# Attention scores as three float32r products, with TensorE in a written order

## The chip, the cores and the metric

The kernel runs on one core of a Trainium2 chip. That core has five engines with their own instruction queues: TensorE (PE; its weight loads are shown apart as PEld), VectorE (DVE), ScalarE (ACT), GpSimd (POOL) and SyncE (SP), which issues the transfers. [...] The metric is the device time of one execution, in microseconds (us).

## The reference, cut to what matters

```python
# q, k, v: (8 batches, 8 heads, 576, 64)
scores = scale * np.matmul(q, k.transpose(0, 1, 3, 2))
mask = block_i >= block_j                       # blocks of 64
scores = np.where(mask, scores, -1000000000.0)
attn = np.exp(scores - max); attn = attn / (sum + 1e-09)
x = np.matmul(attn, v)                          # heads side by side: (8, 576, 512)

h = gelu(x @ w_in); u, v = halves of h          # 512 columns each
v_n = (v - mu) / np.sqrt(var + 1e-06) * g_ln
v_s = np.einsum('ts,bsd->btd', w_sg, v_n) + b_sg[None, :, None]
out = x + (u * v_s) @ w_out
```

All of it is float32.

## The kernel before, in words

Attention is done for a pair of heads at a time: 32 pairs, four to a batch. `load_qk` brings q and k of a pair with the head's 64 values on the rows, head 0 in rows 0 to 63, head 1 in rows 64 to 127, so that the scores of the two heads are products in the two halves of TensorE's rows. A query tile i (five of them) needs the keys up to its own block only. `Scores` makes the scores in four steps (step1: tile 4's first 288 keys and tile 1's 192; step2: tile 4's other 288; step3: tile 3's 448 and tile 0's 64; step4: tile 2's 320). In each, TensorE writes two PSUM banks, one for each head (tile `s`), VectorE takes mask and row maximum (`maximum`, L297), and ScalarE makes the exponentials (`exponent`, L310) into `prob`. `Values` turns the probabilities (`pa`, `pb`, `pc`, `pd`: transposes through PSUM, copied out to `pt`), multiplies them with v (`ob`), turns the reciprocal sums (`pe`), and `normalise` multiplies. The result x is written to DRAM (`spill`) and split in two float32r parts (`split`: xh, xl).

A batch's four pairs done, the feed-forward part runs in pieces: five value strips (`accv`), eight pieces of u (`accu`), eight spatial (`accs`), eight of the output (`acco`). These products are float32r already: each factor is split in a high and a low part, and three products stand for one. Between the value strips and the spatial pieces lies the normalisation (`moments`, `inverse_std`, `centre`, `scale`) on VectorE and GpSimd.

A slot handles pair n's values, pair n + 1's scores, and some pieces of feed-forward work of the batch before (`hole`). The order in which each engine gets its instructions comes from a scheduler that works from the program order and its own estimate of times; `keep_in_program_order` pins single instructions. [...] The output pieces of a batch stand behind the value and u pieces of the next one (`last_o`). In the order printed by the program below, line 85 is every product and line 88 every transpose. Weights come as 64-bit numbers and are turned to float32 by ScalarE and VectorE (`from_f64`), then split.

Of the kernel before, what the change touches and what calls it, by code (L numbers as in the profile page):

```python
# [16 lines left out]
DRAM = bass.MemoryType.DRAM  # L17

# [9 lines left out]
def kernel(  # L28
# [12 lines left out]
    nc = tc.nc  # L41
# [15 lines left out]
    PIN = ""  # L57
# [6 lines left out]
    KINDS = {"x": ("x", 3), "xr": ("r", 2), "xh": ("y", 4), "xl": ("z", 4)}  # L64
# [24 lines left out]

    def copy(e, dst, src):  # L90
        f = {"v": nc.vector.tensor_copy, "a": nc.scalar.copy, "g": nc.gpsimd.tensor_copy}[e]
        return f(dst, src)  # L92
# [8 lines left out]
    def load_qk(n):  # L101
        b, h = PAIRS[n]
        q_f = sp.tile([P, S], F32, tag="q_f", name="q_f", bufs=2)
        k_f = sp.tile([P, S], F32, tag="k_f", name="k_f", bufs=2)
        nc.sync.dma_start(q_f, qT[b, h : h + 2].rearrange("a d s -> (a d) s"))
        nc.sync.dma_start(k_f, kT[b, h : h + 2].rearrange("a d s -> (a d) s"))
        qk[n] = (q_f, k_f)

    def load_v(n):
        b, h = PAIRS[n]  # L110
        v_f = v_bufs[n % 2]
        cols = slice(h * D, (h + 2) * D)
        nc.sync.dma_start(
            v_f[:, : NT - 1, :],
            v[b, : (NT - 1) * P, cols].rearrange("(j p) d -> p j d", p=P),
        )
        nc.sync.dma_start(v_f[:TAIL, NT - 1, :], v[b, S - TAIL :, cols])
        vals[n] = v_f
# [12 lines left out]
    nc.gpsimd.memset(mask, 0.0)  # L131
    nc.gpsimd.memset(mask[:BLK, MW - BLK :], -8.0e9)
    half = cp.tile([P, NT], F32, name="half")
    nc.gpsimd.memset(half, -0.5)
    stats = cp.tile([P, NT, 2], F32, name="stats")
    nc.gpsimd.memset(stats, 1.0)


    for s in (0, 1):
        t = cp.tile([P, NT, 2 * D], F32, name=f"v_f{s}")  # L140
        nc.gpsimd.memset(t[TAIL:, NT - 1, :], 0.0)
        v_bufs.append(t)
    pt0 = []
    for s in (0, 1):
        t = cp.tile([P, 2 * BLK], F32, name=f"pt0_{s}")
        nc.gpsimd.memset(t[BLK:, :], 0.0)
        pt0.append(t)
    prob = []
    for s in range(4):
        row = []  # L150
        for i in range(NT):
            t = cp.tile([P, P * (i + 1) if i else BLK], F32, name=f"prob{s}_{i}")
            if i:
                nc.gpsimd.memset(t[:, EXT[i] :], 0.0)
# [13 lines left out]
    def split_weight(x, dh, dl):  # L168
        nc.scalar.copy(dh, x)
        nc.gpsimd.tensor_tensor(dl, x, dh.bitcast(F32), op=ALU.subtract)  # L170

    def from_f64(raw, dh, dl):
# [8 lines left out]
        nc.scalar.activation(m.bitcast(F32), hi.bitcast(F32), AF.Abs, scale=2.0**-112)  # L181

        nc.vector.tensor_scalar(t, lo, 29, None, op0=ALU.logical_shift_right)
        nc.vector.scalar_tensor_tensor(
            t, hi, 0x80000000, t, op0=ALU.bitwise_and, op1=ALU.bitwise_or
        )
        nc.vector.scalar_tensor_tensor(
# [4 lines left out]
    def load_weight(src, cols, dh, dl):  # L192
# [5 lines left out]
        def fetch(k):  # L198
            if k < len(parts):
                c, fs = parts[k]  # L200
                raws[k] = page(src.dtype, W, "w")
                nc.sync.dma_start(raws[k], src[c * P : (c + 1) * P, fs])
# [3 lines left out]
        for k, (c, fs) in enumerate(parts):  # L206
            fetch(k + 2)
# [3 lines left out]
            else:  # L211
                from_f64(*args)
            yield True

    def load_spatial():
        nc.sync.dma_start(g_bc, g_ln.unsqueeze(0).broadcast_to([P, DH]))
        t = page(F32, S, "w")
        nc.gpsimd.memset(t[BLK:, :DH], 1.0)
        nc.vector.tensor_copy(vone[BLK:, :], t[BLK:, :DH])
        for j in range(NT - 1):  # L220
            t = page(F32, S, "w")
            nc.sync.dma_start(t, w_sgT[j * P : (j + 1) * P, :])
# [5 lines left out]
        for hf in (0, 1):  # L228
            nc.sync.dma_start(t[hf * BLK : (hf + 1) * BLK, :], w_sgT[j * P : S, :])
        t2 = page(F32, S, "w")  # L230
        nc.gpsimd.memset(t2[BLK:, :], 0.0)
        nc.sync.dma_start(t2[BLK : BLK + 1, :], b_sg.unsqueeze(0))
        nc.sync.dma_start(t2[96:97, :], b_sg.unsqueeze(0))
        nc.scalar.copy(ws_h[:, j, :], t)
        nc.gpsimd.tensor_tensor(
            ws_l[:BLK, j, :], t[:BLK, :], ws_h[:BLK, j, :].bitcast(F32), op=ALU.subtract
        )
        nc.scalar.copy(ws_l[BLK:, j, :], t2[BLK:, :])
        nc.vector.tensor_tensor(
# [27 lines left out]
    class Scores:  # L267


        def __init__(self, n):  # L270
            self.q, self.k = qk.pop(n)
            self.sm = sp.tile([P, NT, 2], F32, tag="sums", name="sums", bufs=3)
            nc.gpsimd.memset(self.sm[:, 0, :], 1.0)  # L273
# [6 lines left out]
        def products(self, *parts):  # L280
# [3 lines left out]
            for i, lo, hi in parts:  # L284
                n, rows = QN[i], slice(0, QN[i])
                for a in (0, 1):
                    r = slice(a * D, (a + 1) * D)
                    dst = t[a][rows, off : off + hi - lo]
                    self.where[a, i, lo] = dst
                    mm(dst, self.q[r, QS[i] : QS[i] + n], self.k[r, lo:hi], start=True, stop=True)  # L290
                off += hi - lo

        def maximum(self, a, i, lo, hi):
# [3 lines left out]
            nc.vector.tensor_tensor_reduce(  # L297
# [10 lines left out]
        def exponent(self, a, i):  # L308
            r, e = slice(0, QN[i]), EXT[i]
            nc.scalar.activation(  # L310
# [8 lines left out]
        def step(self, *parts):  # L319
# [4 lines left out]
            for a in (0, 1):  # L324
                for i, lo, hi in parts:
                    if hi == EXT[i]:
                        self.exponent(a, i)
# [10 lines left out]
        def step4(self):  # L338
            self.step((2, 0, EXT[2]))

    TE = {(0, 0): "a", (1, 0): "v", (0, 2): "a", (1, 2): "v", (0, 1): "a", (1, 1): "a"}

    class Values:
# [45 lines left out]
        def inverse(self):  # L389

            r = sp.tile([P, NT * 2], F32, tag="r", name="r", bufs=2)
            nc.vector.tensor_scalar_add(r, self.sm.rearrange("p i a -> p (i a)"), 1e-9)  # L392
            nc.vector.reciprocal(r, r)
            self.rx = sp.tile([P, NT, 2 * D], F32, tag="rx", name="rx", bufs=1)
            nc.gpsimd.tensor_copy(
# [4 lines left out]
        def turn_sums(self):  # L400
# [4 lines left out]
            turn(t[:, 128:256], self.rx[:, 0, :], ident)  # L405
            pt = self.pt0 = pt0[self.n % 2]
            copy("a", pt[:BLK, :], t[:BLK, : 2 * BLK])
            self.rb = sp.tile([P, S], F32, tag="rb", name="rb")
            copy("a", self.rb[:, :BLK], t[:, 128:192])
            t = pbank("pe")  # L410
            for i in range(1, NT):
                turn(t[:, (i - 1) * P : i * P], self.rx[:, i, :], ident)
            copy("a", self.rb[:, BLK:], t)
# [16 lines left out]
        def av1(self):  # L430
            pt = [self.pt.pop((a, 1)) for a in (0, 1)]
            self.av(self.ob[:, 64:512], 1, pt, 0, 448, False, False)
            self.av(self.ob[:, 448:512], 4, pt, 448, 64, False, True)
            self.o0 = self.t4[:, 256 : 256 + BLK]
# [342 lines left out]
```

## Time and profile before

| | us |
|---|---|
| median of the two runs | 1058.67 |
| the two runs | 1051.1, 1066.24 |
| the profiled execution | 1052.77 |
| its span (first to last instruction) | 1050.8 |
| TensorE busy | 964.7 |
| VectorE busy | 465.9 |
| ScalarE busy | 427.0 |
| GpSimd busy | 267.4 |

Busy times are those of the profiled execution. Matmuls are pipelined, so a busy TensorE is not one at its best rate, and how long one product takes in a row of them is read from start to start. The granted clock is the share of its full speed that TensorE's clock had. "Idle before" and a releaser name whose work ended a wait.

### The profile page before, as it was taken

How to read it: one execution, taken by the hardware profiler on the slowest of the kernel's cores; microseconds unless marked ns; L12 is line 12 of the kernel's file. 1: busy time of each engine (PE TensorE's matmuls, PEld its weight loads, DVE VectorE, ACT ScalarE, POOL GpSimd, SP SyncE). 2: the span in 40 equal slices, each digit the busy share in tenths (PEclk: the TensorE clock that was granted, in tenths of full speed). 3: DMA queues.
4: the chain of work that ended last, by engine and by line, in shares of the span. 5: the costliest groups of instructions: out<-in, count | busy, mean ns of one | idle time of the engine just before them, and what ended most of it. 6: DMA issues, size and time to landing. Idle time of an engine off the chain costs nothing.

```text
span 1050.8 us, 15018 instructions
## 1 busy us (share of the span) xinstructions
PE 964.7 (92%) x5554; PEld 690.3 (66%) x5554; DVE 465.9 (44%) x1442; ACT 427.0 (41%) x1122; POOL 267.4 (25%) x341
## 2 busy tenths in 40 slices
PE   8699999998889988999889998899988999889988
PEld 4245767576657765677666776567765577658978
DVE  6855285427334273342722526434263342723333
ACT  5765662562253622536224263243632536322210
POOL 3621064104212042120420303302042020422232
PEclk7799999998989989899878999889989899869999
DMA  7522111112210122101220112211122011112022
GB/s 233 167 91 68 56 56 46 46 46 68 95 34 31 46 68 90 46 22 46 68 80 34 46 47 68 79 35 46 46 68 88 27 44 58 34 39 75 1 90 68
DMA packets 46908, 65.61 MB, mean 62 GB/s; under 512 B 4082, under 2 KB 22514, under 8 KB 46836
## 3 DMA queue, kind: packets, MB, share of 16 engines
q1 hardware_dynamic: 46836, 64.67, 18.8%
q8 instruction: 43, 0.70, 0.3%
q14 instruction: 29, 0.24, 0.1%
HBM read 45.78 MB, written 18.87 MB: 62 GB/s over the span
## 4 chain that ended last, share of the span: by engine, by line
PE 76%; DVE 13%; ACT 3%; DMA 2%; POOL 2%; issue 2%; SPq 1%; DVEq 0%; POOLq 0%; ACTq 0%
PE s L85 12%; PE accs L85 12%; PE acco L85 11%; PE ob L85 11%; PE accv L85 10%; PE accu L85 9%; PE pc L88 3%; PE pb L88 3%; DVE prob L297 3%; PE pa L88 2%; DVE bs L518 2%; DVE xr L635 2%; ACT prob L310 1%; PE pe L88 1%; DMA w<-in_w_in 1%
## 5 line engine op out<-in xcount | busy, mean ns | idle before, releaser
L310 ACT ACTIVATE prob<-prob,negm 128x448 f32<-128x448 f32 (+3 forms) x320 | 177.8, 556 | 235.5 <-DVE negm L297 234.1
L85 PE MATMUL s<-k_f,q_f 64*128 64x288 f32 (+4 forms) x768 | 193.9, 447 | 34.2 <-DVE negm L297 23.7
L297 DVE CUSTOM_DVE_ANT_0 prob<-s,mask 128x288 f32<-128x288 f32 (+2 forms) x320 | 122.2, 424 | 168.9 <-PE s L85 168.8
L85 PEld LDWEIGHTS s<-k_f,q_f 64*128 64x128 f32 (+1 forms) x768 | 88.9, 188 | 102.1 <-issue 40.3
L85 PE MATMUL ob<-pt,v_f 128*64 128x448 f32 (+4 forms) x640 | 129.5, 454 | 11.0 <-ACT pt L92 6.6
L85 PE MATMUL acco<-gh,wo_h 128*128 128x288 f32 x256 | 94.2, 369 | 19.5 <-DVE xr L635 10.9
L273 POOL MEMSET sums<- 128x2 f32 x32 | 4.3, 137 | 353.1 <-DVE r L392 353.1
L611 POOL TENSOR_TENSOR gl<-u,gh 128x288 fp32r<-128x288 f32 x64 | 51.6, 807 | 154.6 <-DVE gh L610 151.9
L85 PEld LDWEIGHTS ob<-pt,v_f 128*64 128x64 f32 x640 | 44.1, 141 | 69.2 <-issue 39.7
L85 PE MATMUL acco<-gl,wo_h 128*128 128x288 f32 x256 | 87.1, 340 | 0.0
L85 PE MATMUL acco<-gh,wo_l 128*128 128x288 f32 x256 | 86.6, 338 | 0.0
L635 DVE TENSOR_TENSOR xr<-acco,xr 128x288 f32<-128x288 f32 x64 | 29.0, 456 | 121.1 <-PE acco L85 113.5
L85 PEld LDWEIGHTS acco<-gh,wo_h 128*128 128x128 f32 x256 | 58.9, 230 | 31.8 <-DVE xr L635 16.6
L85 PE MATMUL accu<-xh,wi_h 128*128 128x288 f32 x256 | 79.1, 309 | 0.0
L85 PE MATMUL accs<-ws_h,vh 128*128 128x288 f32 x256 | 76.8, 303 | 1.5 <-ACT pt L92 1.5
L85 PE MATMUL accs<-ws_h,vl 128*128 128x288 f32 x256 | 75.9, 297 | 0.0
L85 PE MATMUL accu<-xh,wi_l 128*128 128x288 f32 x256 | 75.5, 295 | 0.0
L85 PE MATMUL accu<-xl,wi_h 128*128 128x288 f32 x256 | 75.4, 295 | 0.0
L85 PE MATMUL accs<-ws_l,vh 128*128 128x288 f32 x256 | 75.1, 294 | 0.0
L85 PE MATMUL accv<-wi_h,xh 128*128 128x512 f32 x160 | 66.0, 413 | 0.0
L92 ACT COPY pt<-pa 128x512 f32<-128x512 f32 x32 | 18.6, 581 | 110.8 <-PE pa L88 110.8
L85 PE MATMUL accv<-wi_l,xh 128*128 128x512 f32 x160 | 63.4, 396 | 0.0
(102 smaller groups left out, 1839.8 us busy)
## 6 DMA issues: line engine op xcount, KB each, us to landing
q_f<-in_qT SPq DMA_DIRECT2D x32, 288.0 KB, 2.9
k_f<-in_kT SPq DMA_DIRECT2D x32, 288.0 KB, 3.2
spill<-x SPq DMA_DIRECT2D x32, 288.0 KB, 3.2
xr<-spill SPq DMA_DIRECT2D x32, 288.0 KB, 2.8
out_T<-xr SPq DMA_DIRECT2D x32, 288.0 KB, 2.1
v_f<-in_v SPq DMA_DIRECT2D x32, 256.0 KB, 3.1
w<-in_w_in SPq DMA_DIRECT2D x16, 256.0 KB, 4.7
w<-in_w_out SPq DMA_DIRECT2D x8, 256.0 KB, 3.9
```

What stands on the lines that cost most here:

```text
L85: return pin(nc.tensor.matmul(*a, **k), "P")
L88: return pin(nc.tensor.transpose(out, in_, identity), "P")
L92: return f(dst, src)
L273: nc.gpsimd.memset(self.sm[:, 0, :], 1.0)
L297: nc.vector.tensor_tensor_reduce(self.prob[a][i][r, lo:hi], self.where[a, i, lo], mask[r, MW - (hi - lo) :] if 0 < i and hi == e else mask ...
L310: nc.scalar.activation(self.prob[a][i][r, :e], self.prob[a][i][r, :e], AF.Exp, bias=self.negm[a][r, i : i + 1], scale=-1.0, accum_out=self ...
L518: tc.keep_in_program_order(nc.vector.bn_stats(bs[:rows, :], x))
L611: nc.gpsimd.tensor_tensor(glo[:, ts], x, ghi[:, ts].bitcast(F32), op=ALU.subtract)
L635: nc.vector.tensor_tensor(x[:, ts], acc[:, :SH], x[:, ts], op=ALU.add)
```

## The change

Scores: q and k of a pair are split on the chip, into a float32r high part (VectorE) and the rest (GpSimd), and the score is three products, high by high, high by low, low by high, in one accumulation. For each product the two heads follow one another. The first pair keeps its one fp32 product. q_f and k_f have one buffer each in place of two, and the split of the pair after next stands at the slot's end, so its transfers and the single q_h, k_h, q_l, k_l follow on the step 4 that read the last ones.

Order: `PIN = "P"` pins every TensorE instruction to program order; the other engines are still scheduled. The slot is written anew: one piece of feed-forward work at seven places (PLAN), each score step between a piece and a product with v, the exponentials after the piece behind their step, the side work (`run_side`) in shares of two and three. A batch's output pieces follow its own spatial pieces in the same four slots; those of the last batch but one stay for the end. ScalarE copies `ob` out of PSUM, and VectorE multiplies it with the turned sums where they lie in PSUM; before, ScalarE copied the sums and VectorE read ob. Weight pieces get a tag of their own with two buffers, shared with xr, and are fetched after the piece before is used; x has two buffers in place of three.

```diff
-    PIN = ""
+    PIN = "P"
...
-    KINDS = {"x": ("x", 3), "xr": ("r", 2), "xh": ("y", 4), "xl": ("z", 4)}
+    KINDS = {"x": ("x", 2), "xr": ("r", 2), "raw": ("r", 2), "xh": ("y", 4), "xl": ("z", 4)}
...
+    def split_qk(n):
+        q_f, k_f = qk[n]
+        parts = []
+        for x, name in ((q_f, "q"), (k_f, "k")):
+            hi = sp.tile([P, S], F32R, tag=name + "_h", name=name + "_h")
+            V.tensor_copy(hi, x)
+            parts.append(hi)
+        for x, name, hi in ((k_f, "k", parts[1]), (q_f, "q", parts[0])):
+            lo = sp.tile([P, S], F32R, tag=name + "_l", name=name + "_l")
+            G.tensor_tensor(lo, x, hi.bitcast(F32), op=ALU.subtract)
+            parts.append(lo)
+        q_h, k_h, k_l, q_l = parts
+        qk[n] = [(q_h, k_h), (q_h, k_l), (q_l, k_h)]
...
         for i, lo, hi in parts:
...
-                    mm(dst, self.q[r, QS[i] : QS[i] + n], self.k[r, lo:hi], start=True, stop=True)
+                for y, (q, k) in enumerate(self.terms):
+                    for a in (0, 1):
+                        r = slice(a * D, (a + 1) * D)
+                        mm(
+                            self.where[a, i, lo],
+                            q[r, cols],
+                            k[r, lo:hi],
+                            start=(y == 0),
+                            stop=(y == len(self.terms) - 1),
+                        )
...
         def normalise(self):
...
-            nc.vector.tensor_tensor(x[:, :BLK], self.o0, self.rb[:, :BLK], op=ALU.mult)
-            nc.vector.tensor_tensor(x[:, BLK:], self.ob, self.rb[:, BLK:], op=ALU.mult)
+            copy("a", x[:, BLK:], self.ob)
+            copy("a", x[:, :BLK], self.o0)
+            V.tensor_tensor(x[:, BLK:], self.rp, x[:, BLK:], op=ALU.mult)
+            V.tensor_tensor(x[:, :BLK], self.t4[:, 128:192], x[:, :BLK], op=ALU.mult)
...
-    WS = [2, 5, 7, 8, 3, 2, 1, 1]
+    WS = [6, 7, 7, 4, 3, 2]
...
-    PLAN = ["12211", "12211", "12211", "12222"]
+    PLAN = ["1111111", "1111111", "1111111", "1111112"]
...
+        va.turn0(0)
+        va.turn0(1)
+        hole(g[0])
+        load_share(n, 0)
+        run_side(2)
         if nx:
             nx.step1()
+        va.av0()
+        if nx:
+            nx.exponents(1)
+        va.turn2(0)
+        va.turn2(1)
+        hole(g[1])
+        run_side(2)
         if nx:
             nx.step2()
+        va.av2()
...
-                work.extend([v_, u_, *last_o, s_])
-                last_o[:] = [o_]
+                if b < B - 2:
+                    work.extend([v_, u_, s_, o_])
+                elif b == B - 2:
+                    work.extend([v_, u_, s_])
+                    last_o.append(o_)
+                else:
+                    work.extend([v_, *last_o, u_, s_, o_])
```

How this moves instructions shows at three places. The first is TensorE at step 3 of a slot in the steady part, before (tile `s` is the scores, one number for each head; `ob` the product with v, `pc` transposes; columns are line, operation, out<-in, shape):

```order
L85 MATMUL s_5259<-k_f_4890,q_f_4889 128x448
L85 MATMUL s_5259<-k_f_4890,q_f_4889 64x64
L85 MATMUL s_5260<-k_f_4890,q_f_4889 128x448
L85 MATMUL s_5260<-k_f_4890,q_f_4889 64x64
L85 MATMUL ob_5240<-pt_5230,v_f0_101 64x512
L88 MATMUL pc_5311<-ident_70,prob0_4_116 128x128
```

The same step in the changed program, on TensorE:

```order
L86 MATMUL s_2790<-k_h_2575,q_h_2573 128x448
L86 MATMUL s_2791<-k_h_2575,q_h_2573 128x448
L86 MATMUL s_2790<-k_l_2577,q_h_2573 128x448
L86 MATMUL s_2791<-k_l_2577,q_h_2573 128x448
L86 MATMUL s_2790<-k_h_2575,q_l_2579 128x448
L86 MATMUL s_2791<-k_h_2575,q_l_2579 128x448
L86 MATMUL s_2790<-k_h_2575,q_h_2573 64x64
L86 MATMUL s_2791<-k_h_2575,q_h_2573 64x64
L86 MATMUL s_2790<-k_l_2577,q_h_2573 64x64
L86 MATMUL s_2791<-k_l_2577,q_h_2573 64x64
```

One head's products stood before the other's; now the heads take turns, product by product, and there are three where there was one.

The second place is GpSimd in the normalisation of a batch's value half, from the power (`rs`) to the last low part (`vl`), before:

```order
L537 TENSOR_TENSOR vv_1041<-vv_1041,rs_1184 64x512
L542 TENSOR_TENSOR vl_1545<-vv_1123,vh_1544 128x512
L537 TENSOR_TENSOR vv_1138<-vv_1138,rs_1184 128x512
L542 TENSOR_TENSOR vl_1550<-vv_1138,vh_1549 128x512
L537 TENSOR_TENSOR vv_1173<-vv_1173,rs_1184 128x512
L542 TENSOR_TENSOR vl_1555<-vv_1173,vh_1554 128x512
```

GpSimd there in the changed program (line 99 is every pinned helper; `xh` and `xl` split x, `q_l` and `k_l` are the new low parts, `rx` the reciprocal sums of the next slot):

```order
L99 TENSOR_TENSOR q_l_4100<-q_f_3839,q_h_4094 128x576
L99 TENSOR_TENSOR k_l_4098<-k_f_3840,k_h_4096 128x576
L99 TENSOR_TENSOR vl_4084<-vv_3723,vh_4083 128x512
L99 TENSOR_TENSOR vv_3764<-vv_3764,rs_3783 128x512
L99 TENSOR_TENSOR xh_4140<-x_3766,xh_4140 128x64
L99 TENSOR_TENSOR xl_4141<-x_3766,xh_4140 128x576
L99 TENSOR_TENSOR xh_4442<-x_4075,xh_4442 128x64
L99 TENSOR_TENSOR xl_4443<-x_4075,xh_4442 128x576
L99 MEMSET sums_4747 128x2
L99 COPY rx_4158<-ri_4155 128x640
L99 TENSOR_TENSOR vl_4089<-vv_3764,vh_4088 128x512
```

The low parts of q and k, two splits of x and the next slot's sums now stand between the low parts of the value half.

The third place is SP at the start, before (`w` is a piece of weights):

```order
L105 DMA q_f_66<-in_qT 128x576
L106 DMA k_f_67<-in_kT 128x576
L113 DMA v_f0_101<-in_v 128x4x128
L117 DMA v_f0_101<-in_v 64x128
L105 DMA q_f_155<-in_qT 128x576
L106 DMA k_f_156<-in_kT 128x576
```

SP there in the changed program, from the second piece of weights (`raw`):

```order
L99 DMA raw_244<-in_w_in 128x256
L99 DMA g_bc_151<-in_g_ln 128x512
L99 DMA raw_253<-in_w_in 128x256
L99 DMA raw_315<-in_w_in 128x256
L99 DMA raw_324<-in_w_in 128x256
L99 DMA raw_373<-in_w_in 128x256
L99 DMA raw_425<-in_w_in 128x256
L99 DMA raw_434<-in_w_in 128x256
L99 DMA q_f_201<-in_qT 128x576
L99 DMA k_f_202<-in_kT 128x576
```

The second pair's q and k went out fifth and sixth; now eight pieces of weights stand ahead of them, and the last six of these wait for one of the two buffers.

More of the change, by code (lines that the diff above doesn't have):

```diff
@@ L102, in load_qk @@
         b, h = PAIRS[n]
[L103 to L106, printed above, removed]
+        q_f = sp.tile([P, S], F32, tag="q_f", name="q_f", bufs=1)
+        k_f = sp.tile([P, S], F32, tag="k_f", name="k_f", bufs=1)
+        SP.dma_start(q_f, qT[b, h : h + 2].rearrange("a d s -> (a d) s"))
+        SP.dma_start(k_f, kT[b, h : h + 2].rearrange("a d s -> (a d) s"))
         qk[n] = (q_f, k_f)
+    def split_qk(n):
[11 more added lines that the diff above has]
+        qk[n] = [(q_h, k_h), (q_h, k_l), (q_l, k_h)]
     def load_v(n):
@@ L116, in load_v @@
         )
-        nc.sync.dma_start(v_f[:TAIL, NT - 1, :], v[b, S - TAIL :, cols])
+        SP.dma_start(v_f[:TAIL, NT - 1, :], v[b, S - TAIL :, cols])
         vals[n] = v_f
@@ L339, in step4, with exponents @@
             self.step((2, 0, EXT[2]))
+        def exponents(self, *tiles):
+            for i in tiles:
+                for a in (0, 1):
+                    self.exponent(a, i)
     TE = {(0, 0): "a", (1, 0): "v", (0, 2): "a", (1, 2): "v", (0, 1): "a", (1, 1): "a"}
@@ L577, in u_part @@
                         )
-                last = nc.scalar.copy(u[fo][:, ts], acc[:, :SH]).ins
+                if "A" in PIN:
+                    last = None
+                    V.tensor_copy(u[fo][:, ts], acc[:, :SH])
+                else:
+                    last = A.copy(u[fo][:, ts], acc[:, :SH]).ins
                 if fo * 2 + th == 2 * NC - 1:
@@ L670, in slot @@
         va.inverse()
+        va.turn0(0)
[3 more added lines that the diff above has]
+        run_side(2)
         if nx:
             nx.step1()
-        va.turn0(0)
-        va.turn0(1)
+        va.av0()
[5 more added lines that the diff above has]
+        run_side(2)
         if nx:
             nx.step2()
-        hole(g[0])
-        load_share(n, 0)
-        run_side(4)
-        va.av0()
-        va.turn2(0)
-        va.turn2(1)
+        va.av2()
+        load_share(n, 1)
+        hole(g[2])
+        if nx:
+            nx.exponents(4)
+        run_side(2)
+        va.turn1(0)
+        va.turn1(1)
+        va.turn_first()
         if nx:
             nx.step3()
+        hole(g[3])
+        load_share(n, 2)
+        run_side(2)
+        if nx:
+            nx.exponents(3, 0)
+        va.av1()
+        va.av00()
+        va.turn_sums()
+        if nx:
+            nx.step4()
+        hole(g[4])
+        va.normalise()
+        last = n % (H // 2) == H // 2 - 1
+        if last:
+            for f in pending:
+                f()
+            pending.clear()
+            va.split()
+        run_side(2)
+        if nx:
+            nx.exponents(2)
+        if n + 2 < N:
+            split_qk(n + 2)
+        load_share(n, 3)
+        hole(g[5])
+        run_gelu()
+        run_side(3)
+        hole(g[6])
+        run_side(3)
         for f in pending:
@@ L687, in slot @@
         pending.clear()
-        hole(g[1])
-        run_gelu()
-        load_share(n, 1)
-        run_side(4)
-        va.av2()
-        va.turn1(0)
-        va.turn1(1)
-        va.turn_sums()
-        if nx:
-            nx.step4()
-        hole(g[2])
-        load_share(n, 2)
-        run_side(4)
-        va.av1()
-        va.normalise()
-        hole(g[3])
-        run_gelu()
-        load_share(n, 3)
-        run_side(4)
-        hole(g[4])
-        pending.append(va.split)
+        if not last:
+            pending.append(va.split)
         return nx
@@ L713 @@
     load_v(0)
-    load_qk(1)
     sc = Scores(0)
     sc.step1()
+    sc.exponents(1)
     sc.step2()
+    sc.exponents(4)
     sc.step3()
+    sc.exponents(3, 0)
     sc.step4()
+    sc.exponents(2)
+    load_qk(1)
+    split_qk(1)
     for n in range(N):
@@ L725, in begin @@
                 v_, u_, s_, o_ = feed_forward(b)
-                work.extend([v_, u_, *last_o, s_])
-                last_o[:] = [o_]
-            pending.append(begin)
-    for f in pending:
-        f()
-    work.extend(last_o)
+                if b < B - 2:
[3 more added lines that the diff above has]
+                    last_o.append(o_)
+                else:
+                    work.extend([v_, *last_o, u_, s_, o_])
+            begin()
     while work:
```

165 lines of the change are left out of this document (84 added, 81 removed).

## The prediction

> **What bounds the kernel now.** I read the page first (busy shares and the slices), then stretches of time, then the chain of waits, then the order of time at the score steps.
>
> ```profile
> span 1050.8 us, 15018 instructions
> ...
> PE 964.7 (92%) x5554; PEld 690.3 (66%) x5554; DVE 465.9 (44%) x1442; ACT 427.0 (41%) x1122; POOL 267.4 (25%) x341
> ...
> PEclk7799999998989989899878999889989899869999
> ```
>
> TensorE is busy 92% of the span, nothing else half of it, and its granted clock sags at a regular distance. The stretches (columns: length, busy time of PE, weight loads, DVE, ACT and POOL, clock, DMA share, GB/s) show where:
>
> ```profile
> 0.00:100.60 100.60, 83.38 (x421) 43.65 (x421) 68.05 (x234) 64.02 (x190) 38.52 (x78) 0.85 0.46 146
> 100.60:202.70 102.10, 100.32 (x599) 67.32 (x598) 55.98 (x175) 55.02 (x145) 32.86 (x39) 1.00 0.17 52
> 202.70:253.20 50.50, 49.29 (x312) 36.23 (x312) 19.21 (x64) 24.35 (x63) 5.71 (x9) 1.00 0.18 59
> 253.20:304.40 51.20, 41.68 (x194) 28.57 (x196) 19.90 (x54) 15.09 (x40) 14.98 (x14) 0.80 0.16 53
> ...
> 950.00:1050.80 100.80, 91.17 (x627) 84.32 (x625) 34.56 (x79) 17.44 (x36) 27.70 (x30) 1.00 0.18 56
> ```
>
> The head (batch 0's four pairs) takes 100 us. Then 28 slots, one pair each, take 850 us, 30.4 us a slot. The tail takes 100.8. A batch takes 131 us from one value stage to the next (202.7 to 333.7): 80 us run at full clock with TensorE full, and 51 us (253.2 to 304.4, the stage of output products) run at clock 0.80 with 9.5 us idle. In the period from 100.6 there is no output stage, and four slots take 102.1 us: 25.5 a slot with almost nothing idle. What TensorE waits for in the bad stretches is a PSUM bank that VectorE has not emptied:
>
> ```profile
> PE s L85 <- DVE negm L297: 23.7, 25, 4.1
> ...
> PE acco L85 <- DVE xr L635: 10.9, 20, 1.6
> ```
>
> So the bound is TensorE's own work in most slots, and order in the rest. The four feed-forward stages of a batch cost, from the chain in order of time (start, length, count) in the tail:
>
> ```profile
> 974.30 13.07 PE accv L85 x56
> 987.37 12.73 PE accu L85 x96
> ...
> 1019.61 14.86 PE accs L85 x112
> 1034.47 12.74 PE acco L85 x96
> ```
>
> Together 53.4 us a batch, 13.35 a slot. A float32r product costs 0.133 us at 288 columns (12.73 / 96) and 0.233 at 512 (13.07 / 56): 0.45 ns a column, its weight load hidden.
>
> **The change, part by part.** *Scores.* The order of time shows the fp32 scores in two forms:
>
> ```profile
> 305.56 2.47 PE L85 MATMUL s<-k_f,q_f 64*128 64x448 f32 x8
> 307.96 0.40 PE L85 MATMUL accs<-ws_h,vh 128*128 128x288 f32 x1
> ...
> 311.64 0.29 PE L85 MATMUL accs<-ws_l,vone 128*128 128x288 f32 x1
> 311.87 0.81 PE L85 MATMUL s<-k_f,q_f 64*128 64x320 f32 x4
> ...
> 312.60 1.09 PE L85 MATMUL ob<-pt,v_f 128*64 128x448 f32 x8
> 313.62 0.40 PE L85 MATMUL accs<-ws_h,vh 128*128 128x288 f32 x1
> ```
>
> Step 4 (320 columns) sends the two row halves together: 0.73 us to the next product. Step 3 (448 and 64 columns) sends one head after the other and takes 2.40; at step 4's rate it would take 0.73 x 512 / 320 = 1.17. The first product after a change of row groups stands 0.23 after the last, not 0.13, so a change costs about 0.1. In the full stretch from 100.6 the two attention products took:
>
> ```profile
> L85 PE MATMUL s<-k_f,q_f 64*128 64x288 f32 (+4 forms) x96 | 20.5, 422 | 0.0
> L85 PE MATMUL ob<-pt,v_f 128*64 128x512 f32 (+4 forms) x81 | 19.4, 441 | 0.2 <-DVE negm L297 0.2
> ```
>
> That is 5.1 us of scores a slot. After: six parts (288, 192, 288, 448, 64, 320 columns) times three products, each pair of halves sharing one time. By 0.45 ns a column plus 0.003: 0.13, 0.09, 0.13, 0.205, 0.03, 0.147. No row shows a float32r product in 64 rows, nor one below 288 columns, so the two short ones get an estimate: 0.11 and 0.055, the 0.1 of a change as the least for 128 loaded columns, half of it for 64. Sum 0.78, times 3 is 2.3 us, plus four changes, 2.8. Bounds: 2.3 at the least, a gain of 2.8; 2 x (2.3 + 1.8) = 8.2 if 0.1 stands open at each of the 18 and the halves follow one another, a loss of 3.1. I take 2.8, as both overlaps stand in the rows nearest to it (step 4 for the halves, the feed-forward rate for the loads): minus 2.3 a slot. The first pair stays in fp32.
>
> *Order of TensorE.* The written order keeps the two heads' products adjacent, for the value products (ob) too. Paired, 512 columns take 1.02 us (312.60 to 313.62), so the 1536 of a slot take 3.06 against 19.4 / 4 = 4.85: minus 1.8. The pieces of feed-forward work stand in five places a slot, as before, so the changes between forms stay. The full slot with its share of output products was 25.5 + 12.74 / 4 = 28.7; after, 28.7 - 2.3 - 1.8 = 24.6. Output products move into their own batch's fourth slot, one piece at each place, so the bad stretch goes: each score step now has a piece of 1.6 to 2.8 us behind it while VectorE takes the maxima.
>
> *What is late next.* The split of q and k adds two casts on VectorE and two subtractions on GpSimd a slot, priced by the split of x (xh, xl); GpSimd also carries the normalisation (rs, vv, vl). The last row is for the head, below:
>
> ```profile
> L453 POOL TENSOR_TENSOR xl<-x,xh 128x576 fp32r<-128x576 f32 x32 | 45.7, 1427 | 0.0
> L537 POOL TENSOR_TENSOR vv<-vv,rs 128x512 f32<-128x512 f32 (+1 forms) x40 | 42.5, 1070 | 1.5 <-DVE vv L524 1.1
> L542 POOL TENSOR_TENSOR vl<-vv,vh 128x512 fp32r<-128x512 f32 x32 | 41.6, 1300 | 26.9 <-DVE vh L541 26.9
> ...
> L449 DVE CAST xh<-x 128x576 fp32r<-128x576 f32 x32 | 21.2, 664 | 8.7 <-PE accu L85 8.4
> ...
> L530 POOL TENSOR_TENSOR rs<-rs,half 128x5 f32<-128x5 f32 x8 | 15.0, 1878 | 0.7
> L184 DVE SCALAR_TENSOR_TENSOR w<-w 128x256 uint32<-128x256 uint32 x24 | 13.4, 564 | 0.2
> ```
>
> VectorE gains 1.3 us a slot (41 in all, to 507), GpSimd 2.85 (88, to 356): both far below the span. The split starts when step 4 has read the single q_h and k_h buffers, and the next step 1 comes some four feed-forward pieces (over 6 us) later, against 1.3 + 2.85: hidden, but not in the head, which has no such pieces. Once a batch the cover is thin. In the second slot GpSimd runs from the power to the last vl without a rest: 1.9 + 5 x 1.07 + 4 x 1.3 + 2 x 1.43 (q, k) + 2 x 1.43 (two x) = 18.2 us and several small operations, from about 5 us into the slot (the last moments stand behind step 1's maxima on VectorE): done at 24 or later. The first spatial product wants that tile at 24.6 - 1.9 + 1.3 = 24.0 (a slot less its last piece, 14.86 / 8, and the ten of its 14 products that stand ahead). I take 4 us a batch with the clock it costs: 1.0 a slot. Slot: 25.6. Exponentials move behind the pieces, and ScalarE's two copies of ob replace two of rb: no cost, since ScalarE is busy 41%. The normalising products read PSUM; the banks come free two pieces before the next slot wants them. SP carries the same transfers a slot: q and k of the pair after next wait for GpSimd to have read the single q_f and k_f, most of a slot before their own split, and what stands behind them (v, the spill) is wanted later still.
>
> *Head.* Weight pieces pass through 2 buffers now (up to 10 before), and the second pair's q and k stand on the SP queue behind six loads that wait for such a buffer.
>
> ```profile
> k_f<-in_kT SPq DMA_DIRECT2D x32, 288.0 KB, 3.2
> ...
> w<-in_w_in SPq DMA_DIRECT2D x16, 256.0 KB, 4.7
> ```
>
> A buffer turns over in 3.2 to 4.7 us of landing plus some 1.0 of reading by VectorE and ScalarE (the 0.56 of L184 is the longer of two reads on VectorE); two of them give 2.1 to 2.9 us a piece, and 24 pieces 50 to 70 us from about 9. VectorE has them in its order before the second pair's later maxima, so most of that pair and two whole ones follow, some 12 us each without pieces: head 93 to 114. I take 107, near the slower end, as landings at the start are the slow ones: plus 7.
>
> *Tail.* The spatial stage of batch 6 (14.9) is done in the slots; v, o, u, s, o remain: 66.1 us, plus 8 for waits and the last store: 74. The output stage in it (12.7) is taken off the slots.
>
> **Sum.** 107 + 28 x 25.6 - 12.7 + 74 = 885, plus the 2 us by which the profiled execution (1052.77) exceeds its span: 887. That execution lies 0.6% below the median of the two runs (1058.67), which is within their spread; I say 890.
>
> **Rivals.**
> 1. *Weight loads in the row halves stand open.* In step 4 two fp32 passes over 320 columns take 0.365 us a product; at 0.45 ns a column they would take 0.29, so 0.08 to 0.1 is open there. If each of the 18 products shows 0.1, a slot grows by 1.3 to 1.8 us, and the time is 890 + 28 x 1.6 = 935. The full-array products speak against it: same rows each time, 0.133 us. [...]
> 2. *The two halves do not overlap in float32r.* Then 2.3 us more a slot: 955. Step 4 speaks against it, but for fp32. *Both 1 and 2*: 2 x 1.6 + 2.3 = 5.5 a slot, 1044: the change would then not do what it says, and no change would show.
> 3. *Slower: TensorE stands in its written order.* If every slot had one wait as in 253.2 to 304.4, where 41.7 busy us at clock 0.80 did some 33 us of work in 51.2 (65%), a slot would take 24.6 / 0.65 = 38 and the run 1230. It decides from 31.5 us a slot on, 78%. For it: nothing can be pulled ahead of a late copy any more. Against it: VectorE and ScalarE have over a third of each slot free.
> 4. *The stages move their wait.* Head 130 and 10 us a batch at the first spatial product: 28 x 1.5 + 23 more, 955 alone, near 1000 with rival 1.
>
> **How the numbers follow.** Forecast 0.62 (830 to 930), rivals 1 and 2 0.18, rival 4 with one of them 0.08, rivals 1 and 2 together (no change) 0.05, rival 3 0.07. A measurement of this kernel tells 2% from no change. Faster by over 2%: 0.88; within: 0.05; slower: 0.07. The range 830 to 985 goes from the full slot without waits (28 x 24.6, head 93, tail 70: 839, a little less if short products are cheap) to one overlap missing with a head of 130 (955 + 23 = 978), and leaves out under 2 in 10.
>
> **What would show it.** Scores near 2.8 us a slot of TensorE, halves starting together, pitch 0.13 at 288 columns (not 0.23); the clock at 1.00 through a whole batch with at most one dip, at the first spatial product, with GpSimd's vl as releaser; accv first near 107; the value stages 102 us apart. It is wrong if TensorE waits over 3 us a slot for score maxima or pt copies, or if float32r pairs start one after the other.

## The result and the profile after

The changed kernel takes 943.53 us (942.45 and 944.61), the kernel before 1058.67: a ratio of 0.8912, with a 95% interval of 0.8635 to 0.919. The forecast was 890 (830 to 985). So 115 us went, and 53 of the forecast gain are missing. The page of the profiled execution, with the same rows as before:

```profile
span 940.7 us, 15934 instructions
...
PE 839.8 (89%) x5926; PEld 666.6 (71%) x5926; DVE 525.1 (56%) x1504; ACT 433.9 (46%) x1124; POOL 354.3 (38%) x403
...
PEclk7569799799989999799997999989997999989999
```

TensorE is still the busiest, but its share fell from 92 to 89%: it works less and stands idle more. The clock row has one dip a batch. The stretches show where (columns: length, busy time of PE, weight loads, DVE, ACT, POOL, granted clock, DMA share, GB/s); the first three are head, slots and tail, the last four the slots of one batch, each from its first `pa` transpose to the next slot's:

```profile
0.00:110.10 110.10, 73.81 (x422) 43.30 (x422) 70.04 (x217) 60.47 (x172) 48.19 (x84) 0.72 0.41 127
110.10:869.60 759.50, 699.35 (x5051) 559.82 (x5049) 429.36 (x1229) 360.79 (x931) 285.83 (x298) 0.95 0.20 62
869.60:940.70 71.10, 66.64 (x458) 63.51 (x456) 25.73 (x58) 12.59 (x25) 20.32 (x21) 1.00 0.20 63
...
334.60:362.00 27.40, 27.40 (x178) 20.71 (x177) 10.08 (x35) 14.54 (x36) 3.70 (x5) 1.00 0.28 87
362.00:394.20 32.20, 24.20 (x183) 19.36 (x182) 23.14 (x56) 17.85 (x45) 20.36 (x19) 0.92 0.13 41
394.20:420.80 26.60, 26.60 (x195) 22.60 (x194) 15.02 (x47) 10.37 (x28) 8.45 (x9) 0.91 0.14 36
420.80:445.50 24.70, 24.29 (x194) 20.12 (x192) 14.02 (x43) 9.09 (x27) 8.71 (x12) 1.00 0.33 104
```

Head 110.1 (forecast 107), slots 759.5 (28 x 25.6 - 12.7 = 704), tail 71.1 (74). The miss lies in the slots, and in a batch in its second: 32.2 us, of which TensorE works 24.2. The waits of TensorE (us in all, times, longest) name what it waits for:

```profile
PE accs L86 <- POOL vl L99: 45.1, 15, 4.4
...
PE accs L86 <- DVE vh L99: 10.5, 8, 3.5
```

In order of time TensorE stands at the first spatial products of the batch, three times:

```profile
386.49 0.40 PE L86 MATMUL accs<-ws_h,vl 128*128 128x288 f32 x1 [2.30 <-POOL vl L99]
...
388.26 0.40 PE L86 MATMUL accs<-ws_h,vh 128*128 128x288 f32 x1 [1.24 <-DVE vh L99]
393.06 0.61 PE L86 MATMUL accs<-ws_h,vl 128*128 128x288 f32 x1 [4.40 <-POOL vl L99]
```

What GpSimd does from the power (`rs`) on (start, length, idle time before):

```profile
369.00 2.55 POOL L99 TENSOR_TENSOR rs<-rs,half 128x5 f32<-128x5 f32 x1
...
376.07 1.29 POOL L99 TENSOR_TENSOR vl<-vv,vh 128x512 fp32r<-128x512 f32 x1 [1.88 <-DVE vh L99]
...
381.64 1.43 POOL L99 TENSOR_TENSOR q_l<-q_f,q_h 128x576 fp32r<-128x576 f32 x1 [0.45 <-PE accu L86]
383.47 1.51 POOL L99 TENSOR_TENSOR k_l<-k_f,k_h 128x576 fp32r<-128x576 f32 x1 [0.40 <-DVE k_h L99]
384.95 1.48 POOL L99 TENSOR_TENSOR vl<-vv,vh 128x512 fp32r<-128x512 f32 x1
386.40 1.25 POOL L99 TENSOR_TENSOR vv<-vv,rs 128x512 f32<-128x512 f32 x1
387.61 0.31 POOL L99 TENSOR_TENSOR xh<-x,xh 128x64 fp32r<-128x64 f32 x1
387.88 1.57 POOL L99 TENSOR_TENSOR xl<-x,xh 128x576 fp32r<-128x576 f32 x1
...
391.08 0.71 POOL L99 COPY rx<-ri 128x640 f32<-128x640 f32 x1
391.75 1.25 POOL L99 TENSOR_TENSOR vl<-vv,vh 128x512 fp32r<-128x512 f32 x1
```

The low parts of q and k stand ahead of one vl that TensorE waits for, two splits of x and the next slot's sums ahead of the other. And the wait costs more than its 7.9 us, since the clock stands at 0.50 for 10.3 us, through the last of the three waits and behind it:

```profile
388.90:399.20 10.30, 6.14 (x26) 6.03 (x26) 1.46 (x3) 1.87 (x2) 4.91 (x7) 0.50 0.01 2
```

The scores run as the two rows had it on which the forecast relied. In a score step the halves start together and follow at 0.13 to 0.14 us for 288 columns:

```profile
337.40 0.40 PE L86 MATMUL s<-k_h,q_h 64*128 64x288 f32 x2
337.64 0.29 PE L86 MATMUL s<-k_l,q_h 64*128 64x288 f32 x2
337.78 0.29 PE L86 MATMUL s<-k_h,q_l 64*128 64x288 f32 x2
337.91 0.25 PE L86 MATMUL s<-k_h,q_h 64*128 64x192 f32 x2
...
338.31 0.65 PE L86 MATMUL ob<-pt,v_f 128*64 128x512 f32 x2
```

### The profile page after: what moved, and what is told of

It is laid out like the page before. It is cut to its first block, busy times and chain, and to the rows that moved or that the text cites. A ratio compares the mean times of both kernels' runs of the same rounds, so it can differ in the third digit from the quotient of the medians.

```text
span 940.7 us, 15934 instructions
## 1 busy us (share of the span) xinstructions
PE 839.8 (89%) x5926; PEld 666.6 (71%) x5926; DVE 525.1 (56%) x1504; ACT 433.9 (46%) x1124; POOL 354.3 (38%) x403
## 5 line engine op out<-in xcount | busy, mean ns | idle before, releaser
L99 POOL TENSOR_TENSOR q_l<-q_f,q_h 128x576 fp32r<-128x576 f32 x31 | 44.3, 1429 | 289.5 <-PE s L86 215.1
L86 PE MATMUL ob<-pt,v_f 128*64 128x512 f32 (+4 forms) x640 | 115.6, 459 | 10.4 <-ACT pt L99 9.8
L86 PE MATMUL accs<-ws_h,vh 128*128 128x288 f32 x256 | 83.3, 325 | 10.8 <-DVE vh L99 10.5
L86 PEld LDWEIGHTS accs<-ws_h,vl 128*128 128x128 f32 x256 | 50.6, 198 | 48.9 <-POOL vl L99 48.9
L99 DVE TENSOR_TENSOR u<-accs,u 128x288 f32<-128x288 f32 x64 | 28.6, 448 | 92.8 <-PE accs L86 92.8
L86 PE MATMUL acco<-gh,wo_h 128*128 128x288 f32 x256 | 78.5, 307 | 0.0
L86 PE MATMUL acco<-gl,wo_h 128*128 128x288 f32 x256 | 76.2, 298 | 2.5 <-POOL gl L99 2.5
L86 PEld LDWEIGHTS ob<-pt,v_f 128*64 128x64 f32 x640 | 40.3, 140 | 53.3 <-issue 22.9
L86 PE MATMUL acco<-gh,wo_l 128*128 128x288 f32 x256 | 75.3, 294 | 0.0
L86 PE MATMUL s<-k_h,q_h 64*128 64x288 f32 (+1 forms) x372 | 69.2, 356 | 1.8 <-DVE k_h L99 1.8
L99 ACT COPY pt<-pa 128x512 f32<-128x512 f32 x32 | 18.7, 585 | 110.6 <-PE pa L89 110.5
L89 PEld LDWEIGHTS pb<-ident,prob 128*128 128x128 f32 (+1 forms) x320 | 33.6, 143 | 42.8 <-issue 40.6
L86 PEld LDWEIGHTS accs<-ws_h,vh 128*128 128x128 f32 x256 | 50.5, 197 | 18.4 <-DVE vh L99 14.4
```

The source lines that it names most:

```text
L86: return pin(nc.tensor.matmul(*a, **k), "P")
L89: return pin(nc.tensor.transpose(out, in_, identity), "P")
L99: return lambda *a, **k: pin(f(*a, **k), self.letter)
```

## The experiments

Theory T was that the missing time is GpSimd's queue ahead of the first spatial product. The rivals were VectorE's part of that chain, the scores, and the written order. The four runs of e10 lay between 884.27 and 886.86, the four of e11 between 877.74 and 879.80, but the kernel before, run again beside the experiments, between 1039 and 1060. The other experiments are single runs, so a difference of 1% or less between two of them, such as the 6 us between e3 and e9, is weak by the times alone.

**e1: GpSimd in its written order.**

```diff
-    PIN = "P"
+    PIN = "PG"
```

> GpSimd keeps its written order, nothing else is changed. In a batch's second slot the last two vl then stand ahead of k_l, q_l and of the split of x, where the changed kernel has two xh, two xl, the memset, rx, q_l and k_l between them. Theory T (the missing time is GpSimd's queue in front of the first spatial product): what moves behind the last vl is 2 x 1.46 (xl) + 2 x 0.36 (xh) + 0.8 (memset, rx) + 1.5 + 1.4 (k_l, q_l) = 7.4 us, about the 7.5 us that TensorE stands idle there; the idle falls to under 2 us a batch, the half-clock stretch of 10 us behind it goes, the second slot falls from 32.2 to about 23 and the batch from 110 to about 101: 7 x 9 = 63 us less, about 880 (870 to 895). Rival R1 (the chain is VectorE's vh or the moments, and GpSimd's other work only fills its waits): idle stays above 5 us a batch, 930 to 945. Rival R2 (a pinned GpSimd stands behind operands that are late, and the wait appears elsewhere, at pd, pe or the first score product of the next slot): the spatial wait goes and 3 us a slot come back, 930 to 960.

Measured 909.65. The second slot falls from 32.2 to 27.3 us, the batch from 110 to 104.8, the head is 113.2. TensorE still idles 1.08 + 1.25 + 0.74 us there, since the written order multiplies one vv, waits for VectorE's vh, makes vl, and only then takes the next vv. T has the place right and 34 of the 63 us it expected; the rest is the chain from tile to tile, as R1 had it in part. The waits after:

```profile
PE accs L86 <- POOL vl L99: 13.2, 14, 1.1
...
PE accs L86 <- DVE vh L99: 9.7, 7, 2.2
```

**e2: the low parts of q and k on VectorE.**

```diff
-            G.tensor_tensor(lo, x, hi.bitcast(F32), op=ALU.subtract)
+            V.tensor_tensor(lo, x, hi.bitcast(F32), op=ALU.subtract)
```

> The low parts of q and k are subtracted on VectorE in place of GpSimd; the order of GpSimd is left to the scheduler as in the changed kernel. Theory T: 1.5 + 1.4 us leave GpSimd's queue in front of the first spatial product once a batch, so the idle there falls from 7.5 to about 4.5 us and the half clock may stay: 3 to 5 us a batch, 21 to 35 in all, 908 to 922. VectorE gains 62 subtractions at some 0.7 to 1.2 us (43 to 75 us of busy time, 525 to 570 to 600), hidden. Rival R1 (VectorE is the chain): its queue grows by 1.4 to 2.4 us ahead of the last vh, and the idle grows by as much: 945 to 965.

Measured 934.39: 9 us less, under half of the least that T expected. The wait for vl fell to 24.0 us, that for VectorE's vh rose from 10.5 to 27.5. The second slot takes 31.4. Both engines are links of the chain, and work moved from one to the other stays in it.

**e3: fp32 scores in the written order.** Without the split q_f and k_f get two buffers again.

```diff
-        if n + 2 < N:
-            split_qk(n + 2)
...
-    split_qk(1)
```

> The scores of every pair as one fp32 product (no split of q and k, two buffers of q_f and k_f); the written order of TensorE and all else as in the changed kernel. By the forecast's own price the scores cost 5.1 us a slot in place of the 3.1 measured: 21 slots x 2.0 = 42 more (in a batch's second slot the wait covers it), less 3 us of wait in each of 7 batches as k_l and q_l leave GpSimd: 943.5 + 42 - 21 = 965. If the written order pairs the halves of the long fp32 parts too, at step 4's 0.73 us for 320 columns, the six parts cost 3.7 + 0.4 = 4.1, 1.0 more than now: 943.5 + 21 - 21 = 944. So theory T (the score's form is a small part and the order did the rest): 940 to 970. Rival (the float32r products bring most of the gain, the order little): above 1000.

Measured 917.31, faster than the change, which neither theory had. Three things add up (against the changed kernel): the head takes 96.7 us in place of 110.1; the second slot 29.3 in place of 32.2; and the other slots are as long as before, within 0.5 us at full clock (27.9 against 27.4, 24.6 against 24.7). So the written order pairs the halves of the long fp32 parts too: step 3 (448 and 64 columns), one head after the other before the change, took 2.40 us there and takes 1.26 here. Step 1 takes 1.01 us (347.16 to 348.17) against 0.91 in the rows above (337.40 to 338.31):

```profile
347.16 1.08 PE L86 MATMUL s<-k_f,q_f 64*128 64x288 f32 x8
348.17 0.65 PE L86 MATMUL ob<-pt,v_f 128*64 128x512 f32 x2
...
357.16 1.26 PE L86 MATMUL s<-k_f,q_f 64*128 64x448 f32 x8
```

**e4: one head's three products, then the other's.**

```diff
-                for y, (q, k) in enumerate(self.terms):
-                    for a in (0, 1):
+                for a in (0, 1):
+                    for y, (q, k) in enumerate(self.terms):
```

> In each part of the scores the three products of one head stand together, then the three of the other (in the changed kernel the two heads alternate). Theory T (the alternation is what lets the halves share their time): each of the 18 products takes its columns alone, 2 x 2.3 + 0.4 = 5.0 us and more in place of 3.1: 1.9 us in 21 slots = 40, about 985; with the loads open too (0.1 each at 36 products) up to 3.6 more a slot, 1060. Of a batch's second slot nothing shows. Rival (the halves overlap in whatever order, as each waits for its own rows alone): 940 to 950, scores still 3.1 us a slot.

Measured 953.34, 3 above the rival's range and far under T: the scores take the same 12.5 us of TensorE a batch, measured from start to start, and of the 10 us more 5.5 are in the head. The rows explain it: the products still start in pairs, though they were written three and three, and the pin keeps TensorE to the written order. The queue as the chip got it is in no view here.

```profile
372.61 0.41 PE L86 MATMUL s<-k_h,q_h 64*128 64x288 f32 x2
372.84 0.30 PE L86 MATMUL s<-k_l,q_h 64*128 64x288 f32 x2
372.98 0.30 PE L86 MATMUL s<-k_h,q_l 64*128 64x288 f32 x2
```

**e5: the pin on TensorE taken away.**

```diff
-    PIN = "P"
+    PIN = ""
```

> The changed kernel with its one pin taken away: TensorE's order is the scheduler's again, the float32r scores and everything else stay. Fp32 scores in the written order (e3) gave 917 us, so the score's form cannot be what brought the gain. Theory T (keeping the written order brings it): without the pin most of the gain is gone, 985 to 1050, with more than 20 us of waits of scores on VectorE's maxima (they were 23.7 us before and none in steady slots after). Rival (the places in the slot, not the pin, do it: the scheduler would put the steps about as written): 935 to 960.

Measured 908.46: below both, and 35 us faster than with the pin. TensorE no longer stands at the spatial products; it has no idle time over 0.2 us in a steady batch, and the clock stays up, as its page shows:

```profile
PE 879.8 (97%) x5926; PEld 666.3 (73%) x5926; DVE 545.6 (60%) x1504; ACT 433.8 (48%) x1124; POOL 348.8 (38%) x403
...
PEclk7677999999999999999999999999999999999999
```

One batch, as a stretch of time (columns as above):

```profile
321.10:427.50 106.40, 106.40 (x742) 81.59 (x741) 64.51 (x179) 52.12 (x134) 39.97 (x44) 1.00 0.22 68
```

But it works longer: 106.4 us a batch, against 101.8 in e1. From start to start, the value products `ob` take 16.8 us a batch here and 11.8 with the pin, as the heads fall apart. The pin saves 5 us a batch there and gives back 7.9 of idle time and some 3 of half clock.

**e6: fp32 scores, GpSimd in its written order** (e3 and e1 together).

> Fp32 scores (e3) with GpSimd kept in its written order as well. In e3 TensorE idles 0.6 + 4.4 us at the first spatial products of each batch, its second slot takes 29.3 us and its clock is halved for 6.8 us behind that. Theory T: in written order the split of x, memset and rx (3 to 4.5 us) stand behind the last vl, so the idle falls to 0.5 to 1.5 us, the second slot to 23 to 25 and the third from 26.9 to about 25.5: 5 to 7 us in each of 7 batches, 917 - 42 = 875 (865 to 885). Rival (what is left of the wait is the chain vv, vh, vl from tile to tile between GpSimd and VectorE, as the 3.3 us left in e1 suggest): idle 3 us or more, 890 to 905.

Measured 881.01, T, with a little more idle time than it had: 0.96 + 0.95 us a batch, second slot 25.7, third 24.8 to 26.4. Without q_l and k_l GpSimd's last vl ends 25.0 us into the slot, for 26.1 in e1; with GpSimd's order left to the scheduler the same step was worth 3 us (28.1 in e3 for 31.0).

**e7: the first spatial piece one place later** (on e1).

```diff
-    PLAN = ["1111111", "1111111", "1111111", "1111112"]
+    PLAN = ["1111111", "1111110", "1111112", "1111112"]
```

> Float32r scores, GpSimd in its written order (e1: 909.65 us), and the first spatial piece moved from the end of a batch's second slot to the front of its third, which then holds eight. In e1 TensorE still idles 1.1 + 1.25 + 0.95 us there. The piece now comes some 2 us later (the pa transposes, 1.9 us, stand ahead of it). Theory T: idle falls to about 1 us a batch and no half clock follows; second slot about 21, third about 27, 98 to 99.5 a batch in place of 104.8: 5.3 to 6.8 in each of 7, 862 to 873. Rival (the gap is not the distance but the pairing vv, vh, vl, which just starts later): 885 to 905. The head stays at 113.

Measured 920.36: slower than e1, outside both. The idle time at the spatial products is 1.84 + 0.95 us. TensorE comes there only 1.6 us later in the slot than in e1, and the chain ends 0.6 later, since the next slot's pt copy now stands on VectorE ahead of the last vh. And a new wait follows: q_l, which GpSimd makes behind the last vl, is late for the next slot's first score step.

```profile
PE accs L86 <- DVE vh L99: 13.7, 7, 2.6
...
PE s L86 <- POOL q_l L99: 8.5, 12, 0.9
```

The third slot takes 33.6 us at a clock of 0.90, for the 27 that T had.

**e8: e6 and e7 together.**

> e6 and e7 together: fp32 scores, GpSimd pinned, first spatial piece in the third slot. Theory T: no wait at the first spatial product is left, batches of 27.9 + 20.9 + 27.4 + 24.6 = 100.8; head 97, tail 71, one output stage of 14.6 less in the last batch: 97 + 7 x 100.8 - 14.6 + 71 + 2 = 861 (850 to 870). Against e7 this weighs the two sides of the split: 0.5 us a slot more on TensorE (14 to 16 us), some 15 us less in the head; within 10 us of e7. Rival (the split still costs GpSimd time that TensorE waits for): e8 over 15 us below e7.

Measured 873.66, 3.7 above T's bound. One gap of 0.95 us a batch is left, the clock stays up, the head takes 95.5. The rival came on the split of q and k: e8 is 47 us below e7, over its 15. Of these 18 lie in the head.

**e9: fp32 scores and no pin.**

> Neither of the change's two named parts: fp32 scores and no pin on TensorE. What stays of the change is the slot as written anew (score steps and feed-forward pieces alternating in seven places, output products in their own batch, exponentials behind the pieces). It closes the square with the changed kernel (943.5), fp32 with the pin (e3, 917.3) and float32r without it (e5, 908.5). Theory T1 (the places in the slot made the gain; the score's form is worth the 0.5 us a slot that e3 showed, about 14 us, against some 10 us in the head): 900 to 925. Theory T2 (without the pin fp32 halves fall apart as they did before, where scores took 24.6 us of TensorE in a batch and not 13.2, so the float32r form is worth 10 us a batch when TensorE's order is free): 908 + 7 x 10 - 10 = 968, 945 to 990. Theory T3 (pin or form, either one, is needed at all): near 1040.

Measured 923.82, T1, near its upper end. The four corners, in us:

| | fp32 scores | three float32r products |
|---|---|---|
| TensorE left to the scheduler | 923.8 (e9) | 908.5 (e5) |
| TensorE in the written order | 917.3 (e3) | 943.5 (the change) |
| TensorE and GpSimd in it | 881.0 (e6) | 909.65 (e1) |

Each of the change's two named parts alone gains 6 or 15 us on e9; together they lose 20, as the pinned TensorE stands behind a GpSimd that the split has made later. The gain of e9 over before, 122 us (1045.5 in the same session), belongs to all the rest of the change together: the slot as written anew, the output pieces in their own batch, ScalarE's copies of ob and the new buffers. They were not tried apart.

**e10: pins on both, float32r from the fifth pair on, the later spatial piece, and each vv multiplied ahead of the vl of the tile before.**

```diff
+        def scaled(k):
+            if k == 0:
+                scale(seq[0])
+            if k + 1 < NT:
+                scale(seq[k + 1])
+            parts(seq[k])
...
-        if n + 2 < N:
+        if 4 <= n + 2 < N:
             split_qk(n + 2)
```

> What the runs so far suggest, together: TensorE and GpSimd in their written order, float32r scores from the fifth pair on (the head's pairs in fp32, so that their splits don't stand between the weight pieces), the first spatial piece in a batch's third slot, and the scaling written so that the next vv is multiplied before the vl of the tile before it (in e7 GpSimd stood 1.9 + 0.5 + 1.9 + 1.2 us behind VectorE's vh, one tile after the other). Theory T (all that is missing in e7 is that wait and the head): no idle over 0.3 us at the spatial stage, no half clock after the head; batches of 27.4 + 20.5 + 26.9 + 24.0 = 98.8; head 97 to 106 (the first fp32 pairs have one buffer of q and k); tail 71 and the last batch without its output stage: 101 + 7 x 98.8 - 14.6 + 71 + 2 = 851 (842 to 862). Rival (q_l and k_l still come late for the next slot's first score product, as in e7, where it waited 0.7 us a batch, and the clock halves there): 870 to 890. Before: 1050.

Measured 885.48, a ratio of 0.8484 (0.8426 to 0.8542) to before: the rival. The spatial wait is gone, and k_l and q_l are late instead:

```profile
PE s L86 <- POOL q_l L99: 8.2, 9, 1.2
PE s L86 <- POOL k_l L99: 3.1, 7, 0.9
```

The head takes 101.7 us (e1: 113.2), so it was the split of its pairs that filled it.

**e11: e8 with the same scaling.**

> e8 (fp32 scores, TensorE and GpSimd in written order, first spatial piece in the third slot: 873.66) with the scaling written so that the next vv is multiplied before the vl of the tile before it. In e10 the same edit moved the wait from the spatial products to q_l and k_l; here there is no split of q and k, so nothing stands behind the last vl that TensorE wants soon. Theory T (GpSimd's queue is then off TensorE's path altogether): the 0.95 us idle a batch that e8 has left at the spatial stage goes, the third slot falls from 28.3 to 27.3, 7 us in all: 867 (862 to 871), and over 15 us below e10. Rival (e8's rest is not GpSimd's): 871 to 876.

Measured 878.71, a ratio of 0.8399 (0.8278 to 0.8521) to before, but 5 us above e8. No spatial wait is left, as T had it, but waits on ScalarE's exponentials rose (`pa` on prob from 12.7 to 21.5 us, `ob` on pt from 9.1 to 17.6). The third slot takes 29.4 in place of 28.3. One VectorE row from each shows where it begins, e11 first, e8 second:

```profile
351.46 1.50 DVE L99 CAST vh<-vv 128x512 fp32r<-128x512 f32 x1 [0.80 <-POOL vv L99]
```

```profile
349.63 0.43 DVE L99 CAST vh<-vv 128x512 fp32r<-128x512 f32 x1 [1.03 <-POOL vv L99]
```

On GpSimd in e11, beside the first of them:

```profile
351.39 1.28 POOL L99 TENSOR_TENSOR vl<-vv,vh 128x512 fp32r<-128x512 f32 x1
```

GpSimd now hardly rests. Two of VectorE's vh casts take 1.50 us; each began while a vl ran on GpSimd and ended 0.3 us after it (see the last section). So the maxima of the last score step, behind them, end 22.9 us into the slot in place of 20.7.

**e12: e11 with the pieces bunched.**

```diff
-    PLAN = ["1111111", "1111110", "1111112", "1111112"]
+    PLAN = ["1020211", "1020210", "1020212", "1020212"]
```

> e11 with the feed-forward pieces bunched again: none between score step 1 and step 2 and none between step 3 and step 4, two at the next place each; the same pieces in each slot. It prices the spreading alone, in a kernel whose TensorE otherwise waits for nothing. Between two steps then stand only the attention products and transposes, some 2.5 us of TensorE, against 1.6 us of maxima and 0.7 of a pt copy on VectorE and a like copy on ScalarE. Theory T (the spreading is what hides the maxima and copies): 1 to 3 us idle a slot with waits of s on negm and of ob on pt, and half clock where they add up: 895 to 950. Rival (the attention work between the steps is cover enough, and the spreading is worth little): 865 to 880.

Measured 860.68, the fastest of all and 18 us below e11, better than the rival expected. Steady batches take 100.9 us against 103.3, with the clock at 1.00; idle time in them falls from 2.4 to 1.3 us, as the exponentials come in time again (`pa` on prob 10.5 us in place of 21.5), and pieces that stand two together change form less often (u 13.5 to 13.1 us a batch from start to start, spatial 15.6 to 15.2), while the value products grow from 11.8 to 12.7. The head is 4.8 us shorter. How the rest divides wasn't tried. Spread pieces hide nothing here that attention work doesn't hide.

## Why the prediction was right, and where it wasn't

The range held and the direction was right. The sum was 53 us short. One term, a wait, accounts for most of that; two others were off as well, and gains that it had not counted hid them.

*The wait at the first spatial product* is the mis-sized term: "I take 4 us a batch with the clock it costs". It is 7.9 us of idle time (2.30 + 1.24 + 4.40) and some 3 us of half clock (the spatial products take 18.7 us a batch from start to start, 15.6 in e11, where the clock stays up). The place, the engine and the releaser were right, and the half-clock stretch was in the text, but the chain was counted too short and TensorE's arrival too late. The forecast had GpSimd done at 24 us into the slot or later, and TensorE there at 24.0; GpSimd is done at 31.0 (393.00 less 362.00) and TensorE first stops at 22.2. Its reading "without a rest" is what failed: GpSimd starts at 6.7 (forecast: about 5), works 20.4 us, and stands another 3.9 in between, mostly for VectorE's vv, vh and k_h. Batches take 109.5 to 110.9 us (115 the first) against a forecast of 102.4, and the slots without the wait are nearly as forecast: 110.9 less 7.9 less 3 is 100, 25.0 a slot for 24.6. That agreement is partly luck: the next two terms bring 2.8 us a slot, not 4.1. Most of the rest came from what the forecast held as it was in the stretch from 100.6: its 1.8 us of idle time went, and from start to start a batch's transposes `pc` fell from 6.1 to 4.7 us and its spatial products, where the clock stays up, from 16.8 to 15.6. Five middle batches 7.6 too long, the first 12.6 and the last 5 make the 55 us of the slots. e1 and e6 took 34 and 36 us (943.5 to 909.65, 917.3 to 881.0) off by GpSimd's order alone.

*Scores, minus 2.3 a slot.* From start to start the scores took 4.5 us a slot in the full stretch before and 3.1 after: minus 1.4. The forecast took 5.1 from a busy time, and each busy stretch runs on after the next product has started (at step 4 0.81 us, for 0.73 from start to start). Nor is the change of type what gains: in the written order fp32 scores take 3.6, so 0.9 of the 1.4 is pairing and 0.5 is float32r. The row of step 4 said so: at 0.73 us for 320 columns in pairs, the 1600 columns of a slot come to 3.65.

*Order, minus 1.8 on the value products.* From start to start 4.35 us a slot in the full stretch before, 2.94 after: minus 1.4, and without the pin it is 4.2 (e5). This term is the pin's, as forecast. That the pin is also what makes TensorE stand idle was rival 3's mechanism, and it came, in one slot of four: 32.2 us there, over the 31.5 from which it would have decided had every slot been so.

*The stretch of output products.* It went, as forecast, but not by the pin: without pin and split (e9) a batch has no idle time either. Which part of the new slot did it wasn't tried; e12 shows only that spreading the pieces wasn't needed.

*Head, 107 for 110.1.* Nearly right for a wrong reason, and by the forecast's own sign, the first accv near 107, less near: it comes at 113.5. The two weight buffers and the loads on SP were named; with the same two buffers and no split, e3's head takes 96.7, and e10's 101.7 with one buffer of q and k. The split of the head's pairs, named only as not hidden there, costs 11 to 13 us (113.2 less 101.7, 110.1 less 96.7). *Tail, 74 for 71.1*, right.

*Rival 1* (loads open) is out: three products in the same 64 rows follow at 0.13 and 0.14 us for 288 columns, as the full-array products do (0.133). *Rival 2* (halves one after another) is out too: 337.40 starts both. *Rival 4* was right in its half on the spatial product (10 us a batch), wrong on the head.

## What to carry to other kernels

Here the pin on TensorE was worth the pairing it kept (5 us a batch on the value products) and cost the waits that its order no longer walked around (7.9 us a batch, and some 3 of half clock): price both, and pin or shorten the engine it waits for as well. Before work is given to an idle engine, find the one place in the period where that engine is ahead of the critical one, and count the whole queue there, with the waits inside it, not its share of the span. Take the cost of products that overlap from start to start, and test the parts of a change apart: here each of two parts gained alone, and together they lost.

## What the runs showed of the hardware

*In e4 each row half kept its own order.* There the second head's first product starts within 0.01 us of the first head's, ahead in time of two products that stand before it in the written order; the next pairs likewise. If the queue was as written, the products in these rows started in its order within each half only, not across the two. The halves did not overlap in every order: before the change, with four products of one head ahead of the other's, step 3 took 2.40 us, about twice the 1.26 of e3.

*In these runs VectorE's casts waited out a GpSimd operation.* The cast of k takes 1.09 us on average in the changed kernel, where GpSimd subtracts q_l beside it, and 0.46 in e1, where GpSimd waits for that cast:

```profile
L99 DVE CAST k_h<-k_f 128x576 fp32r<-128x576 f32 x31 | 33.9, 1093 | 0.0
```

```profile
L99 DVE CAST k_h<-k_f 128x576 fp32r<-128x576 f32 x31 | 14.3, 460 | 0.0
```

It isn't slowed evenly. In the changed kernel's slot above q_l runs on GpSimd from 381.64 to 383.07, and the cast ends at 383.39, 0.32 us after it:

```profile
382.25 1.14 DVE L99 CAST k_h<-k_f 128x576 fp32r<-128x576 f32 x1
```

The same holds throughout: in the 14 profiles 370 casts (q_h, k_h, xh, vh) began while a GpSimd operation of 0.6 us or more still had over 0.05 us to run, and each ended 0.28 to 0.39 us after that operation's end; the other 954 took 0.36 to 0.59 us. So it matters here which of the two starts first. What makes the cast wait was not shown, and the forecast left the wait out. It explains part of VectorE's 525 us where 507 were forecast, but little of the long chain: in the slot above GpSimd waits 0.40 us for k_h.

*In e8 a wait of 0.95 us cost no clock.* An idle 0.95 us a batch brought no dip there: the third slot took 28.3 us, 0.9 over the 27.4 expected without a wait. In the changed kernel 7.9 us brought one of 10.3 us, at 0.50. In e6, 1.9 us brought a dip of 3.4 us in some batches (third slot 26.4) and none in others (24.8).
